# The sign of converted float64 weights: written by a Prelu in place of operations of its own

## The chip, the cores and the metric

The kernel runs on 1 core of a Trainium2 chip, in one launch. Times are device microseconds (us): the median of 3 runs is 590.7 us (590.65 to 592.02). A profile was taken of one execution; its span, from the first instruction to the last, is 589.4 us. Engines are named as in the profile: PE is TensorE (PEld its weight loads), DVE is VectorE, ACT is ScalarE, POOL is GpSimd, SP is SyncE, which issues most DMAs.

## The reference

Three layers follow one another. All sizes are fixed, and the two MLPs' weights arrive as float64.

```python
# 1: retention with decay, batch 2, 8 heads, 768 positions, 64 channels, blocks of 64
intra = einsum(qb, kb) * Dmask ; intra = einsum(intra, vb)
inter = einsum(qb * lam_pow, kv_state)
out   = intra + inter
kv_state = lam**64 * kv_state + einsum(kb * rev_pow, vb)
# 2: MLP, x is 1536 x 512, w_in 512 x 2048, w_out 2048 x 512
h = x @ w_in ; r = maximum(h, 0) ; x = (r * r) @ w_out
# 3: gated MLP, w_gate and w_val 512 x 1536, w_out 1536 x 512
out = (sigmoid(x @ w_gate) * (x @ w_val)) @ w_out
```

## The kernel before, in words

**Weights.** The weights are cut into 68 units of 128 x 512 numbers: 2 for each of the 16 blocks of the first MLP (w_in, w_out), 3 for each of the 12 blocks of the second (gate, value, w_out). A unit arrives as float64, as pairs of 32-bit words (tile `raw`, 512 KB). [...]

A conversion has an ACT part, `conv_act` (L145), and a DVE part, `conv_dve` (L168). ACT scales the high word, read as float32, by 2^-112 with a Copy (tile `j`, L155): that moves the exponent so that three bits are free below the sign. It also scales the low word into an integer `r`, the bits that the high word lacks (L163). DVE shifts `j` left by 3 into `m` (L186), which loses the sign, and at the end adds `m` and `r` into the float32 unit `u` (L181). For the sign there are two ways:

- Without `sign`: DVE takes the top bit of `j` and joins it to `m` with one more operation over the unit (L189). Where the unit is to be negated (`flip`, the gate and value units of even blocks of the second MLP) the shift also sets the top bit (L196) and the join is an exclusive or.
- With `sign=True`: DVE has no such operation. ACT writes `r` in two halves instead: the low 16 bits from the low word (L159) and the high 16 bits as a float16 made from the high word scaled by 2^-60 (L161), which holds the sign alone. 16 of the 68 units are converted in this way, all of them early.

**Stages.** One stream of instructions per engine, in the order in which the code is written (a manual schedule). First retention, 4 of 6 chunk pairs, with PE kept busy by filler matmuls at its start (to 43 us). Then `step_1` for 16 blocks f of the first MLP on the first 512 tokens (to 150 us), with the other retention pairs between. Then the first MLP's other tokens, as seven products per 2 x 2 block (L678, to 224 us), its second matmul (L1066, to 311 us), `step_2` for 12 blocks of the second MLP on the first 512 tokens (to 410 us), and the rest, again by seven products (L678, L995).

PE keeps precision by splitting: every factor is a rounded high part and a low rest (`whi`, `wlo`), so a product is 3 groups of 4 matmuls of 512 columns. In `step_1(f)` PE runs `mm_in(f)` (12 matmuls, L472: whi by xh, then wlo by xh, then whi by xl) and `mm_out(f-1)` (12, L486: gh by whi, gh by wlo, gl by whi). ACT rounds the next block's two units (`whi`, L458), squares the activated block (`r`, L503; `g`, L504), rounds it (`gh`, L516), and does the ACT part of two conversions. DVE makes the rests (`wlo`, L460; `gl`, L518) and the DVE part of two conversions; `weave` (L205) puts the conversion's operations and these rests on DVE's queue in turn, one of each. From f = 8 on, work for the next stage is mixed in at places set by a running clock of PE's planned work: `combine_x` makes sums and splits of the activations (`t` L577, `xch` L561, `xcl` L564), `prepare_a` those of weights (`as` L642 to L645, `ah` L651, `al` L657).

Conversions run in retention and `step_1` (34 units on ACT), beside the second matmul of the first MLP (24, `convert`) and in the first part of `step_2` (the rest). Every conversion's last operation leads to a store, and every `conv_act` with `more` to the next load of `raw`, both on SP's queue.

Of the kernel before, what the change touches and what calls it, by code (L numbers as in the profile page):

```python
# [7 lines left out]
F32 = mybir.dt.float32  # L8
F32R = mybir.dt.float32r
AF = mybir.ActivationFunctionType  # L10
ALU = mybir.AluOpType
# [27 lines left out]
def retention_moe_kernel(  # L39
# [24 lines left out]
    nc = tc.nc  # L64
# [6 lines left out]
    I32 = mybir.dt.int32  # L71
# [11 lines left out]
    def unit(name, dt=F32):  # L83
        return up.tile([P, 512], dt, tag="u", name=name)
# [8 lines left out]
    def at(pos, fn):  # L93
        agenda.append((pos, len(agenda), fn))
# [40 lines left out]
    def load_w(n):  # L135
        for _ in range(min(n, len(to_load))):
            ph, f, u = key = to_load.pop(0)
            t = wp.tile([P, 512, 2], I32, tag="w", name="raw")
            src = (w1 if ph == 1 else w2)[f, u].bitcast(I32)
            nc.sync.dma_start(out=t, in_=src.rearrange("p (n two) -> p n two", two=2))  # L140
            raw_t[key] = t

    ready = []

    def conv_act(more=True, sign=False):  # L145

        if not to_conv or to_conv[0] not in raw_t:
            return  # L150
        key = to_conv.pop(0)
        t = raw_t.pop(key)
        j = unit("j")
        r = unit("r", I32)
        nc.scalar.activation(j, t[:, :, 1].bitcast(F32), AF.Copy, scale=2.0**-112)  # L155
        low = t[:, :, 0].bitcast(mybir.dt.uint32)
        if sign:
            parts = r.bitcast(mybir.dt.int16).rearrange("p (n two) -> p n two", two=2)
            nc.scalar.activation(parts[:, :, 0], low, AF.Copy, scale=2.0**-29)  # L159
            top = parts[:, :, 1].bitcast(mybir.dt.float16)  # L160
            nc.scalar.activation(top, t[:, :, 1].bitcast(F32), AF.Copy, scale=2.0**-60)  # L161
        else:
            nc.scalar.activation(r, low, AF.Copy, scale=2.0**-29)  # L163
        ready.append((key, j.bitcast(I32), r, sign))
        if more:
            load_w(1)

    def conv_dve():  # L168

        if not ready:  # L170
            return []
        key, j, r, sign = ready.pop(0)
        ph, f, u = key
        flip = ph == 2 and u < 2 and f % 2 == 0
        m = unit("m", I32)
        w = unit("u")
        if ph == 1:
            w_t[key] = w

        def last():  # L180
            nc.vector.tensor_tensor(out=w.bitcast(I32), in0=m, in1=r, op=ALU.add)  # L181
            n_stored[0] += 1
            at(clock[0] + 4.0, lambda: nc.sync.dma_start(out=w32[ph][f, u], in_=w))

        ops = [
            lambda: nc.vector.tensor_scalar(  # L186
                out=m, in0=j, scalar1=3, scalar2=None, op0=ALU.logical_shift_left
            ),
            lambda: nc.vector.scalar_tensor_tensor(  # L189
                out=m, in0=j, scalar=-(2**31), in1=m, op0=ALU.bitwise_and,  # L190
                op1=ALU.bitwise_xor if flip else ALU.bitwise_or,
            ),
            last,
        ]
        if flip:
            ops[0] = lambda: nc.vector.tensor_scalar(  # L196
                out=m, in0=j, scalar1=3, scalar2=-(2**31),
                op0=ALU.logical_shift_left, op1=ALU.bitwise_or,
            )
        if sign:  # L200
            assert not flip
            ops.pop(1)
        return ops

    def weave(a, b):  # L205

        for i in range(max(len(a), len(b))):
            for ops in (a, b):
                if i < len(ops):
                    ops[i]()  # L210

    def run(ops):
        weave(ops, [])
# [79 lines left out]
    def new_xr():  # L293
        for t in (1, 2):
            xr[t] = xp.tile([P, 4, TB], F32, tag=f"xr{t}", name=f"xr{t}")
# [156 lines left out]
    def split_w(ph, f):  # L452
        ops = []
        for u in range(2 if ph == 1 else 3):
            src = w_t.pop((ph, f, u))
            hi = unit("whi", F32R)
            lo = unit("wlo", F32R)
            nc.scalar.copy(hi, src)  # L458
            ops.append(
                lambda lo=lo, src=src, hi=hi: nc.vector.tensor_tensor(  # L460
                    out=lo, in0=src, in1=hi, op=ALU.subtract
                )
            )
            split_t[ph, f, u] = (hi, lo)
        return ops
# [26 lines left out]
    def stage_a(ph, f):  # L492
        accs = []
        for u in range(ph):
            accs.append(bank())
            mm_in(accs[u], split_t.pop((ph, f, u)))
        return accs
# [23 lines left out]
    def stage_b(ph, f, g):  # L521
        nf = NF1 if ph == 1 else NF2
        if f == 0:
            accs[ph] = [bank() for _ in range(4)]
        mm_out(accs[ph], split_t.pop((ph, f, ph)), g, f == 0, f == nf - 1)
# [565 lines left out]
    def attend(half):  # L1091
        what, k = SLOTS.get(half, (None, 0))
        if what == "scores":
            att_scores(k)
            passed(SCORES)
            if k < NCH - 1:
                load("q5 v5" if k == 10 else "q12 v11")
            return lambda: (att_keys(k), run(att_prep(k)))
        if what == "out":
            pair = PAIRS[k]  # L1100
            for c in pair:
                att_decay(c, nc.gpsimd)
            att_uv(pair)
            att_out(pair)
            for c in pair:
                kv_t.pop(c)
            passed(REST)
            return lambda: [f() for c in pair for f in att_state(c) + att_x(c)]
        return lambda: None

    def step_1(f):

        acc = stage_a(1, f)
        n = PACE[f] if len(to_conv) + len(ready) > 3 * NF2 else 0
        weave(conv_dve() if n > 0 else [], split_w(1, f + 1) if 0 < f < NF1 - 1 else [])
        if rest:
            rest.pop()()
        if n > 0:
            conv_act()
        attend(2 * f)()  # L1120
        if prev:
            stage_b(*prev.pop())
        last = attend(2 * f + 1)
        gs, ops = split_g(elem(1, f, acc))
        weave(conv_dve() if n > 1 else [], ops)
        for m in range(1, n):
            if m > 1:
                run(conv_dve())
            conv_act(True, f < 10)
        last()  # L1130
        prev.append((1, f, gs))

# [24 lines left out]
    with tc.manual_schedule():  # L1157
# [4 lines left out]
        warm_up(WARM)  # L1162
        decay_rows()
        new_xr()
        conv_act(False, True)
        load(NEXT)
        run(conv_dve())
        conv_act(False, True)
        run(conv_dve())
        att_scores(0)  # L1170
        warm_up(FILL[0])
# [6 lines left out]
        ops = [op for c in PAIRS[0] for op in att_prep(c)]  # L1178
        run([ops[1], ops[0], ops[2], ops[3]])
        query(SEQ_CH + 1, qk_t[SEQ_CH + 1][:, 0, :])  # L1180
        for k in range(LEAD):
            pair, nxt = PAIRS[k], PAIRS[k + 1]
            att_out(pair)
            if k:
                att_uv(pair)
            if not k:
                x = [f for c in pair for f in att_x(c)]
                att_scores(nxt[0])
                att_uv(pair)
                att_scores(nxt[1])  # L1190
            elif k + 1 < LEAD:
                for c in nxt:
                    att_scores(c)
            else:
                att_scores(nxt[0])
            for c in pair:
                kv_t.pop(c)
            load(LOOP[k])
            if k < 2:
                conv_act(False, True)  # L1200
            for c in pair:
                run(att_state(c))
            if k + 1 < LEAD:
                for c in nxt:
                    att_decay(c, nc.scalar)
                more = [op for c in nxt for op in att_prep(c)]
                for c in nxt:
                    att_keys(c)
                if not k:
                    run(x + more)  # L1210
                else:
                    run(more)
                    x = [f for c in pair for f in att_x(c)]
                    if k + 2 == LEAD:
                        run(split_w(1, 0))
                    run(x)
                if k < 2:
                    run(conv_dve())
                else:
                    conv_act(False, True)  # L1220
            else:
                run([f for c in pair for f in att_x(c)])
                run(split_w(1, 1))
                conv_act(False, True)
                run(conv_dve())
                att_keys(nxt[0])
                late = att_prep(nxt[0])
                rest.append(lambda: run(late))
            flush()
# [120 lines left out]
```

## Time and profile before

| | |
|---|---|
| median of 3 runs | 590.7 us |
| span of the profiled execution | 589.4 us |
| PE busy | 576.1 us, 98% |
| DVE busy | 474.0 us, 80% |
| ACT busy | 366.9 us, 62% |
| POOL busy | 47.6 us, 8% |
| chain that ended last, by engine | PE 80%, DVE 9%, ACT 4%, DMA 3%, issue 3% |
| TensorE clock granted | 1.00 in every slice |

The profiled execution has no total of its own beside its span; 590.7 - 589.4 = 1.3 us is what lies around the span against the median run. The chain is the work that ended last, followed back from the end: its shares say which engine was waited for, which busy time alone does not. A wait is put down to the engine and line whose signal came last.

### The profile page before, as it was taken

To read this page: it belongs to the slowest core of one execution; us is meant where nothing else is said; L and a number is where in the kernel's file an instruction comes from. 1 tells how busy PE (TensorE), PEld (TensorE's weight loads), DVE (VectorE), ACT (ScalarE), POOL (GpSimd) and SP (SyncE) were. 2 spreads that over 40 slices of the span, in tenths; PEclk is the share of its full clock that TensorE was granted. 3 is DMA by queue.
4 is the path that set the end of the run, shared out by engine and by line. 5 is a ranking of instruction groups with operands and counts; after the bars stand their busy time and mean duration, and the time that the engine had idled before them with its cause. 6 is when DMAs were issued, how large, how long until landed. Compare 5 with 4: busy or idle time off the path is not lost.

```text
span 589.4 us, 9045 instructions
## 1 busy us (share of the span) xinstructions
PE 576.1 (98%) x3172; PEld 471.7 (80%) x3172; DVE 474.0 (80%) x732; ACT 366.9 (62%) x605; POOL 47.6 (8%) x48
## 2 busy tenths in 40 slices
PE   9899999999999999999999999999999999999996
PEld 8788888767888888888888887888887888878885
DVE  2789896899788868988777788985678877789974
ACT  4679999997656557756467645544545554475470
POOL 1751100000000000000000000022012110000000
PEclk9999999999999999999999999999999999999999
DMA  7999896783253297999978878994547678488681
GB/s 260 413 405 376 311 310 216 226 293 105 71 189 134 108 304 263 413 408 413 404 273 289 307 246 272 339 305 102 174 89 205 187 229 233 153 320 307 205 304 72
DMA packets 69008, 150.83 MB, mean 256 GB/s; under 512 B 7137, under 2 KB 14305, under 8 KB 68962
## 3 DMA queue, kind: packets, MB, share of 16 engines
q1 hardware_dynamic: 64656, 144.34, 68.8%
q0 software_dynamic: 3360, 3.93, 4.5%
q10 hardware_dynamic: 946, 1.97, 1.0%
q8 instruction: 25, 0.41, 0.3%
q14 instruction: 21, 0.17, 0.1%
HBM read 106.43 MB, written 42.21 MB: 252 GB/s over the span
## 4 chain that ended last, share of the span: by engine, by line
PE 80%; DVE 9%; ACT 4%; DMA 3%; issue 3%; POOL 0%; DVEq 0%; SPq 0%; ACTq 0%
PE p L678 28%; PE p L1066 15%; PE p L472 15%; PE p L486 10%; PE p L995 8%; DMA gr<-gs 2%; PE p L315 2%; PE p L400 2%; DMA decay<-w_dram 1%; DVE at L350 1%; PE p L383 1%; DVE m L189 1%; PE p L411 1%; DVE gq L862 1%; DVE xcl L564 1%
## 5 line engine op out<-in xcount | busy, mean ns | idle before, releaser
L678 PE MATMUL p<-xch,ah 128*128 128x512 f32 x280 | 110.0, 393 | 1.0 <-ACT s L687 0.5
L678 PE MATMUL p<-xcl,ah 128*128 128x512 f32 x280 | 109.1, 390 | 0.0
L678 PE MATMUL p<-xch,al 128*128 128x512 f32 x280 | 109.1, 390 | 0.0
L678 PEld LDWEIGHTS p<-xch,ah 128*128 128x128 f32 x280 | 52.6, 188 | 15.3 <-ACT s L687 3.5
L687 ACT COPY s<-p 128x512 f32<-128x512 f32 x60 | 35.2, 588 | 43.8 <-PE p L678 43.7
L678 PEld LDWEIGHTS p<-xch,al 128*128 128x128 f32 x280 | 52.6, 188 | 11.0
L678 PEld LDWEIGHTS p<-xcl,ah 128*128 128x128 f32 x280 | 52.6, 188 | 10.6
L995 PE MATMUL p<-gq,wq 128*128 128x512 f32 x252 | 57.7, 390 | 1.0 <-DVE wq L952 1.0
L692 DVE TENSOR_TENSOR c<-p,s 128x512 f32<-128x512 f32 x60 | 41.2, 687 | 19.4 <-PE p L678 19.0
L995 PEld LDWEIGHTS p<-gq,wq 128*128 128x128 f32 x252 | 47.2, 188 | 11.4 <-DVE wq L952 1.6
L155 ACT ACTIVATE j<-raw 128x512 f32<-128x512 f32 x68 | 45.7, 672 | 12.9 <-issue 5.3
L181 DVE CUSTOM_DVE_ANT_0 u<-m,r 128x1024 uint16<-128x1024 uint16 x68 | 49.6, 729 | 4.7 <-ACT r L161 1.7
L460 DVE TENSOR_TENSOR wlo<-u,whi 128x512 fp32r<-128x512 f32 x68 | 46.0, 708 | 6.2 <-ACT whi L458 5.0
L1066 PE MATMUL p<-g2h,whi 128*128 128x512 f32 x128 | 49.8, 389 | 0.0
L1066 PE MATMUL p<-g2l,whi 128*128 128x512 f32 x128 | 49.8, 389 | 0.0
L1066 PE MATMUL p<-g2h,wlo 128*128 128x512 f32 x128 | 49.8, 389 | 0.0
L472 PE MATMUL p<-xh,wlo 128*128 128x512 f32 x160 | 43.8, 395 | 3.8 <-DVE wlo L460 3.8
L472 PE MATMUL p<-xh,whi 128*128 128x512 f32 x160 | 43.2, 392 | 0.0
L472 PE MATMUL p<-xl,whi 128*128 128x512 f32 x160 | 42.8, 390 | 0.0
L163 ACT ACTIVATE r<-raw 128x512 int32<-128x512 uint32 x52 | 34.5, 663 | 8.2 <-PE p L1066 4.9
L472 PEld LDWEIGHTS p<-xh,wlo 128*128 128x128 f32 x160 | 29.4, 188 | 12.6 <-DVE wlo L460 6.9
L458 ACT CAST whi<-u 128x512 fp32r<-128x512 f32 x68 | 37.9, 615 | 0.5 <-PE p L472 0.5
(129 smaller groups left out, 1048.3 us busy)
## 6 DMA issues: line engine op xcount, KB each, us to landing
raw<-in_w SPq DMA_DIRECT2D x68, 512.0 KB, 6.4
w<-u SPq DMA_DIRECT2D x68, 256.0 KB, 5.1
u<-w SPq DMA_DIRECT2D x52, 256.0 KB, 5.1
a<-w SPq DMA_DIRECT2D x20, 512.0 KB, 4.1
g<-g SPq DMA_DIRECT2D x32, 256.0 KB, 4.4
g<-g SPq DMA_DIRECT2D x16, 512.0 KB, 7.6
gr<-gs SPq DMA_DIRECT2D x24, 256.0 KB, 5.6
kv<-in_kv SPq DMA_DIRECT2D x11, 512.0 KB, 10.4
```

What stands on the lines that cost most here:

```text
L155: nc.scalar.activation(j, t[:, :, 1].bitcast(F32), AF.Copy, scale=2.0**-112)
L163: nc.scalar.activation(r, low, AF.Copy, scale=2.0**-29)
L181: nc.vector.tensor_tensor(out=w.bitcast(I32), in0=m, in1=r, op=ALU.add)
L458: nc.scalar.copy(hi, src)
L460: lambda lo=lo, src=src, hi=hi: nc.vector.tensor_tensor(out=lo, in0=src, in1=hi, op=ALU.subtract)
L472: nc.tensor.matmul(acc, lhsT=a[:, kk * P : (kk + 1) * P], rhs=b[:, kk, :], start=i == 0, stop=i == 11,)
L486: nc.tensor.matmul(acc[e], lhsT=a[:, e * P : (e + 1) * P], rhs=b, start=first and i == 0, stop=last and i == 2,)
L678: nc.tensor.matmul(acc, lhsT=w[:, col, kk * P : (kk + 1) * P], rhs=x[:, kk, :], start=start and i == 0, stop=stop and i == 5, skip_group_c ...
L687: nc.scalar.copy(s, acc)
L692: nc.vector.tensor_tensor(out=c, in0=acc, in1=s, op=ALU.add)
L995: nc.tensor.matmul(acc[k], lhsT=a[:, wn], rhs=block_of(b, gn), start=first and n == 0, stop=last and n == 3 * len(group) - 1,)
L1066: nc.tensor.matmul(acc[e, t], lhsT=a[:, e * P : (e + 1) * P], rhs=b[:, t, :], start=first and i == 0, stop=last and i == 2,)
```

## The change

The scaling of the high word becomes a Prelu: for words at or above zero it multiplies by the scale, for negative ones by the scale and by `alpha`. With `alpha` = 2^32 the exponent of a negative word lands 32 higher, so that after the shift left by 3 the top bit is set, and the rest of the bits are the same as for a positive word. For units to be negated the two are exchanged (scale 2^-80, `alpha` 2^-32). DVE's join (L189) goes for all 52 units that had it, ACT's third operation (L161) for the 16 that had that, and with it the strided 16-bit write (L159) becomes the plain one (L163). `conv_dve` returns two operations, so in `weave` the last one (`u`) stands one place earlier.

```diff
-    def conv_act(more=True, sign=False):
+    def conv_act(more=True):
...
-        nc.scalar.activation(j, t[:, :, 1].bitcast(F32), AF.Copy, scale=2.0**-112)
+        ph, f, u = key
+        flip = ph == 2 and u < 2 and f % 2 == 0
+        nc.scalar.activation(
+            j, t[:, :, 1].bitcast(F32), AF.Prelu,
+            scale=2.0**-80 if flip else 2.0**-112, alpha=2.0**-32 if flip else 2.0**32,
+        )
         low = t[:, :, 0].bitcast(mybir.dt.uint32)
-        if sign:
-            parts = r.bitcast(mybir.dt.int16).rearrange("p (n two) -> p n two", two=2)
-            nc.scalar.activation(parts[:, :, 0], low, AF.Copy, scale=2.0**-29)
-            top = parts[:, :, 1].bitcast(mybir.dt.float16)
-            nc.scalar.activation(top, t[:, :, 1].bitcast(F32), AF.Copy, scale=2.0**-60)
-        else:
-            nc.scalar.activation(r, low, AF.Copy, scale=2.0**-29)
-        ready.append((key, j.bitcast(I32), r, sign))
+        nc.scalar.activation(r, low, AF.Copy, scale=2.0**-29)
+        ready.append((key, j.bitcast(I32), r))
...
-        ops = [
+        return [
             lambda: nc.vector.tensor_scalar(
                 out=m, in0=j, scalar1=3, scalar2=None, op0=ALU.logical_shift_left
             ),
-            lambda: nc.vector.scalar_tensor_tensor(
-                out=m, in0=j, scalar=-(2**31), in1=m, op0=ALU.bitwise_and,
-                op1=ALU.bitwise_xor if flip else ALU.bitwise_or,
-            ),
             last,
         ]
```

Line numbers fall by 15 in the changed kernel behind this place (L460 becomes L445); `j` is L157, `r` L162, the shift L184, `u` L179. No instruction of PE, POOL or SP moves. DVE's queue has 660 rows before and 608 after, ACT's 501 and 485; both have two ACT_TABLE_LOADs, one at the start and one ahead of the first Sigmoid.

The first place is ACT's queue in `step_1(8)`, where a conversion of the early kind stands (r_1519 of the unit j_1518, between the rounding gh of block 8 and the whi of block 10). Before:

```order
L503 ACTIVATE r_1505<-p_1458 128x512
L504 ACTIVATE g_1506<-r_1505 128x512
L516 CAST gh_1509<-g_1506 128x512
L155 ACTIVATE j_1518<-raw_1386 128x512
L159 ACTIVATE r_1519<-raw_1386 128x512
L161 ACTIVATE r_1519<-raw_1386 128x512
L458 CAST whi_1542<-u_1444 128x512
```

The same place on ACT after:

```order
L488 ACTIVATE r_1483<-p_1436 128x512
L489 ACTIVATE g_1484<-r_1483 128x512
L501 CAST gh_1487<-g_1484 128x512
L157 ACTIVATE j_1495<-raw_1366 128x512
L162 ACTIVATE r_1496<-raw_1366 128x512
L443 CAST whi_1518<-u_1424 128x512
```

Everything behind the conversion moves up by one instruction.

The second place is DVE's queue in `step_1(13)`, from block 12's rest gl_1791 over the sums `as` of the next stage's weights to the two rests `wlo` of block 14 and the conversion u_1828 woven with them. Before:

```order
L186 TENSOR_SCALAR m_1793<-j_1766 128x512
L518 TENSOR_TENSOR gl_1791<-g_1787,gh_1790 128x512
L189 SCALAR_TENSOR_TENSOR m_1793<-j_1766,m_1793 128x512
L181 ISA u_1794<-m_1793,r_1767 128x1024
L642 TENSOR_TENSOR as_1822<-a_1710 128x256
...
L186 TENSOR_SCALAR m_1827<-j_1799 128x512
L460 TENSOR_TENSOR wlo_1830<-u_1723,whi_1829 128x512
L189 SCALAR_TENSOR_TENSOR m_1827<-j_1799,m_1827 128x512
L460 TENSOR_TENSOR wlo_1833<-u_1754,whi_1832 128x512
L181 ISA u_1828<-m_1827,r_1800 128x1024
```

The same place on DVE after:

```order
L184 TENSOR_SCALAR m_1763<-j_1736 128x512
L503 TENSOR_TENSOR gl_1761<-g_1757,gh_1760 128x512
L179 ISA u_1764<-m_1763,r_1737 128x1024
L627 TENSOR_TENSOR as_1791<-a_1682 128x256
...
L184 TENSOR_SCALAR m_1796<-j_1768 128x512
L445 TENSOR_TENSOR wlo_1799<-u_1695,whi_1798 128x512
L179 ISA u_1797<-m_1796,r_1769 128x1024
L445 TENSOR_TENSOR wlo_1802<-u_1725,whi_1801 128x512
```

Both joins are gone, and the conversion's last operation (u_1797 after, u_1828 before) now stands ahead of the second `wlo`, where the join stood.

## Rows read from the trace of the kernel before

**Rows 1.** Windows: stretch, PE, PEld, DVE, ACT, POOL busy us (count), clock, DMA.

```profile
43.00:95.00 52.00, 52.00 (x392) 42.34 (x388) 47.02 (x78) 48.69 (x85) 7.16 (x6) 1.00 0.89 322
95.00:141.50 46.50, 43.17 (x191) 32.88 (x183) 40.57 (x66) 42.18 (x70) 0.00 (x0) 1.00 0.67 224
```

**Rows 2.** Chain that ended last, in retention: start us, us, what.

```profile
23.75 1.28 DVE at L350 x2
```

**Rows 3.** Timeline, PE: start us, us, engine, line, operation, tiles, shape, count.

```profile
106.21 1.07 PE L472 MATMUL p<-xh,whi 128*128 128x512 f32 x4
111.65 1.07 PE L472 MATMUL p<-xh,whi 128*128 128x512 f32 x4
144.56 0.39 PE L678 MATMUL p<-xch,ah 128*128 128x512 f32 x1
```

**Rows 4.** Waits from 95 to 141.5 us: total us, times, longest.

```profile
PEld p L472 <- DVE wlo L460: 5.4, 5, 2.0
ACT xch L561 <- DVE t L577: 1.2, 2, 0.9
```

**Rows 5.** Groups by line and shape, whole span: busy us, mean ns, idle before.

```profile
L155 ACT ACTIVATE j<-raw 128x512 f32<-128x512 f32 x68 | 45.7, 672 | 12.9 <-issue 5.3 <-DMA raw<-in_w 3.3 <-PE p L1066 2.4
L458 ACT CAST whi<-u 128x512 fp32r<-128x512 f32 x68 | 37.9, 615 | 0.5 <-PE p L472 0.5
L687 ACT COPY s<-p 128x512 f32<-128x512 f32 x60 | 35.2, 588 | 43.8 <-PE p L678 43.7
L163 ACT ACTIVATE r<-raw 128x512 int32<-128x512 uint32 x52 | 34.5, 663 | 8.2 <-PE p L1066 4.9 <-PE p L486 2.9 <-PE p L472 0.3
L651 ACT CAST ah<-as 128x1024 fp32r<-128x1024 f32 x20 | 20.9, 1046 | 1.1 <-DVE as L645 1.1
L159 ACT ACTIVATE r<-raw 128x512 int16<-128x512 uint32 x16 | 12.6, 786 | 0.2 <-PE p L486 0.2
L161 ACT ACTIVATE r<-raw 128x512 f16<-128x512 f32 x16 | 12.4, 772 | 0.0
L503 ACT ACTIVATE r<-p 128x512 f32<-128x512 f32 x16 | 9.4, 589 | 0.0
L367 ACT ACTIVATE tt<-S,G 128x64 f32<-128x64 f32 x24 | 6.0, 335 | 3.7 <-DVE S L430 3.7
```

**Rows 6.** Groups by line, 95 to 141.5 us.

```profile
L155 ACT ACTIVATE j<-raw 128x512 f32<-128x512 f32 x12 | 8.1, 673 | 0.0
L161 ACT ACTIVATE r<-raw 128x512 f16<-128x512 f32 x2 | 1.5, 771 | 0.0
L189 DVE SCALAR_TENSOR_TENSOR m<-j,m 128x512 int32<-128x512 int32 x9 | 6.2, 684 | 0.0
```

**Rows 7.** Timeline, ACT in `step_1`.

```profile
102.42 0.78 ACT L161 ACTIVATE r<-raw 128x512 f16<-128x512 f32 x1
103.06 1.12 ACT L458 CAST whi<-u 128x512 fp32r<-128x512 f32 x2
...
122.39 1.05 ACT L561 CAST xch<-t 128x1024 fp32r<-128x1024 f32 x1 [0.86 <-DVE t L577]
...
133.57 0.62 ACT L516 CAST gh<-g 128x512 fp32r<-128x512 f32 x1
```

**Rows 8.** Timeline, DVE and the PE that waits for it.

```profile
115.32 0.69 DVE L518 TENSOR_TENSOR gl<-g,gh 128x512 fp32r<-128x512 f32 x1 [0.45 <-ACT gh L516]
...
132.48 0.68 DVE L460 TENSOR_TENSOR wlo<-u,whi 128x512 fp32r<-128x512 f32 x1
...
133.22 0.74 PE L472 MATMUL p<-xh,wlo 128*128 128x512 f32 x2 [1.62 <-DVE wlo L460]
```

**Rows 9.** Timeline, PE and DVE in `step_2`.

```profile
349.24 1.07 PE L472 MATMUL p<-xh,whi 128*128 128x512 f32 x4
...
358.41 1.89 DVE L460 TENSOR_TENSOR wlo<-u,whi 128x512 fp32r<-128x512 f32 x3
...
361.12 1.08 PE L472 MATMUL p<-xh,whi 128*128 128x512 f32 x4
```

More of the change, by code (lines that the diff above doesn't have):

```diff
@@ L171, in conv_dve @@
             return []
-        key, j, r, sign = ready.pop(0)
+        key, j, r = ready.pop(0)
         ph, f, u = key
-        flip = ph == 2 and u < 2 and f % 2 == 0
         m = unit("m", I32)
@@ L188, in conv_dve @@
             ),
-            lambda: nc.vector.scalar_tensor_tensor(
-                out=m, in0=j, scalar=-(2**31), in1=m, op0=ALU.bitwise_and,
-                op1=ALU.bitwise_xor if flip else ALU.bitwise_or,
-            ),
             last,
         ]
[L195 to L203, printed above, removed]
     def weave(a, b):
@@ L1128, in step_1 @@
                 run(conv_dve())
-            conv_act(True, f < 10)
+            conv_act(True)
         last()
@@ L1164, in retention_moe_kernel @@
         new_xr()
-        conv_act(False, True)
+        conv_act(False)
         load(NEXT)
         run(conv_dve())
-        conv_act(False, True)
+        conv_act(False)
         run(conv_dve())
@@ L1199, in retention_moe_kernel @@
             if k < 2:
-                conv_act(False, True)
+                conv_act(False)
             for c in pair:
@@ L1219, in retention_moe_kernel @@
                 else:
-                    conv_act(False, True)
+                    conv_act(False)
             else:
@@ L1223, in retention_moe_kernel @@
                 run(split_w(1, 1))
-                conv_act(False, True)
+                conv_act(False)
                 run(conv_dve())
```

## The prediction

> **What bounds the kernel now.** I read the stages first (windows), then PE's starts (timeline), then who was waited for (waits), then ACT's and DVE's queues where PE waits. PE is busy 576 of 589 us, so only time that PE loses can be won. Where the conversions run, it loses time in two stretches.
>
> The pace of PE without loss: `mm_in` of block 10 starts at 106.21 us, that of block 11 at 111.65, 24 matmuls later [rows 3]. That is 5.44 us per block, 0.227 us per matmul, 2.72 us for 12. From 111.65 us to the first product of the next stage at 144.56 lie 5 `mm_in` and 5 `mm_out`, 120 matmuls, 27.2 us at that pace; they took 32.9. **PE loses 5.7 us here**, nearly all of it waiting for `wlo` [rows 3, 4]. In 43 to 95 us it loses nothing, with DVE busy for 47.0 and ACT for 48.7 of 52 us [rows 1]; what is saved there buys no time.
>
> The second stretch is in `step_2`. From 349.24 to 361.12 us there are four thirds of its block: 48 matmuls, 10.9 us at the pace, 11.9 taken. **1.0 us is lost**, most of it at the `wlo` of 358.41 [rows 9].
>
> In retention the chain goes through DVE's products with the decay [rows 2], which wait for scores from PE; none of the five conversions of that stage is in it, so I count nothing there. Between 144.6 and 349 us, and from 361 us to the end, PE waits for no part of a conversion.
>
> **Part by part.** *The join on DVE.* 52 instructions go, at 0.684 us each [rows 6]; 35.6 us of DVE's time, of which nine lie in the first stretch.
>
> *The third operation on ACT.* 16 go. The next start behind one is 0.64 us later (102.42 to 103.06 [rows 7]), and the write ahead of it gets 0.12 us shorter (786 to 663 ns [rows 5]): 0.76 us per unit. Two of these units are converted after 95 us [rows 6]; the one at 102.42 and the second near 109 give 1.5 us.
>
> *The Prelu itself.* No Prelu is in the trace. Nearest rows: a Relu from PSUM takes 589 ns and a copy from PSUM 588 [rows 5] (L503 and L687), so another function costs nothing there, and I take the 672 ns of today's Copy on line 155 [rows 5]. Above: an operand that each row of the tile fetches. L367 has one, 335 ns for 64 columns; the casts of 512 and 1024 columns (615, 1046) give 0.842 ns per column and 184 ns fixed, so 64 columns would take 238, and the operand costs 97 ns [rows 5]. Below: 57 ns less, if the Prelu got down to the cast's 615. For the 12 conversions of the first stretch [rows 6] that is +1.2 and -0.7 us of ACT's time.
>
> The Trainium skill (ScalarE: Activation LUTs, What ACT_TABLE_LOAD costs) states 93 ns for an operand held in a tile and none for a number in the instruction; the trace's 97 ns agrees. The diff gives `alpha` as a number, so by that rule the term is 0; if the engine treats it as a tile's operand all the same, it is 12 times 93 ns, 1.1 us, and the sum below 1.1 us smaller.
>
> *The place of `u`.* It stands ahead of the second `wlo` now. That `wlo` is the rest of the block's output weights, which `mm_out` uses a whole `mm_in` later; and 0.73 us of `u` in place of 0.69 of the join costs it 0.04 us. `u` waits for an `r` that ACT wrote ahead of the `whi` that the first `wlo` needs. No wait is added. Stores and loads on SP follow `u` and ACT as before, as many of them.
>
> *First stretch, ACT.* ACT is the engine to watch: of 46.5 us it is busy for 42.2 [rows 1], the rest being a little at its start and end, and two waits for DVE's `t`, 1.2 us together [rows 4]. So from 95 us on its queue sets the pace. The rounding `gh` of block 13 starts at 133.57 and ends at 134.2. Earlier by: 1.5 us for the two operations, and 0.86 for the wait at 122.39, which goes since DVE is then far ahead [rows 7]. (The other wait, 0.35 us, stays: ACT gets there earlier by as much as DVE.) Together 2.3 to 2.4 us; `gh` is there at 131.9.
>
> *First stretch, DVE.* From the `gl` at 115.32 to the `wlo` of block 14 at 132.48 DVE never rests, and five joins stand between, each worth the 0.61 us to the next start or a little more [rows 6, 8]: 3.1 us. The `gl` waits for ACT's `gh` and comes 1.4 earlier with ACT. So that `wlo` starts at 128.0 and is done at 128.7. PE would want it 4 matmuls behind the start of that `mm_in`: 111.65 + 6 x 2.72 = 127.97, + 0.91 = 128.9. Just in time, and the 1.62 us wait at 133.22 [rows 8] is gone; the earlier `wlo`s have more room.
>
> *What is late next.* After 7 groups of 12, at 111.65 + 19.04 = 130.69 us, PE wants `gh` of block 13 for `mm_out(13)`, and gets it at 131.9: it waits 1.2 us, for ACT. Behind it `mm_out(13)`, `mm_in(15)` and `mm_out(14)` run without a stop (ACT's last conversion is over), 8.16 us, to 140.1 us, and the next stage starts then; 144.56 before. The first stretch gives 4.5 us, less 0.1 for the restart: **4.4**.
>
> *Second stretch.* DVE alone is late there, by 1.0 us, and three joins stand ahead of the last `wlo` between 348 and 356 us, worth 1.9 us: **1.0**, all that is lost.
>
> *Sum.* 5.4 us off the span of 589.4: 584.0. With the 1.3 us that lie between span and median, 590.7 - 5.4 = **585.3 us**.
>
> **Rivals.**
> - *All the loss goes.* ACT's delay at `gh` of block 13 is only 1.2 us, less if the Prelu is a little shorter or ACT has 0.76 us more by a third early unit. Then 5.7 + 1.0 = 6.7: 584.0 us. Against: the ACT queue has next to no idle time left.
> - *The Prelu costs what a fetched operand costs.* ACT has 1.2 us more to do in the first stretch, and as its queue paces PE, PE gets it all: 5.4 - 1.2 = 4.2, 586.5 us. For: Prelu has one number more than Copy uses. Against: the 589 and 588 of [rows 5].
> - *Only ACT's own advance counts.* If some wait of DVE on ACT that I left out paces PE at each block, PE advances by 2.3 us as ACT does, and 1.0 in the second stretch: 587.4 us.
> - *It makes no difference*: the chain that PE waits for closes again over something else, a load of `raw` above all, that comes in time only because PE is late today; 590 us. Against: between 95 and 141 us no wait is for a DMA.
> - *Slower: the Prelu takes a second pass.* If the negative side cost another pass over the tile, each `j` would take 0.57 us more. In the first stretch 12 of them put 6.8 us on the engine that paces it; from 43 to 95 us 17 of them put 9.7 us on ACT, where 9 early units give back 6.8 and only 3.3 us are idle [rows 1], so some 1.6 us of it reaches PE. 585.3 + 6.8 + 1.6 = 593.7 us. It turns slower from 5.4 / 12 = 0.45 us per Prelu. For: nothing but that no Prelu is in the trace; against: Relu, which also tells the signs apart, at a copy's price.
>
> That the change does not do what it says is no rival: the joins and the third operations are out of the two queues, and there are as many table loads as before.
>
> **How the numbers follow.** Forecast 0.52; all the loss 0.13; fetched operand 0.15; ACT's advance only 0.10; no difference 0.06; second pass 0.04. The range reaches from all the loss, 583.8, to beyond ACT's advance, 588.0: it leaves out the last two and slips of the others. What a measurement can tell from no change is 0.3%, 1.8 us, so faster means under 588.9: the first four, 0.90; within, 0.06; slower, 0.04.
>
> **What would show it.** Right: no group for L189 or L161; `j` at 0.66 to 0.69 us; in 95 to 137 us PE's waits for `wlo` under 1 us, and one wait of about 1 us for `gh` near 131; the first L678 near 140 us; no wait for `wlo` near 355. DVE some 36 us less busy, ACT some 14. Wrong: `j` over 0.75 us; PE still waiting for `wlo` for 2 us or more in that stretch; or a new wait behind 140 us, for weights or activations that came early enough only because PE was late.

## The result, and the profile after

| | before | changed |
|---|---|---|
| median | 590.9 us (590.65 to 592.02, 4 runs) | 584.3 us (584.02 to 587.14, 4 runs) |
| span of the profiled execution | 589.4 us | 582.4 us |
| DVE busy | 474.0 us | 436.8 us |
| ACT busy | 366.9 us | 356.5 us |

The ratio is 0.9901, with a 95% interval from 0.9877 to 0.9924 (the two medians alone give 0.9888): 1.0% faster. The forecast was 585.3 us, its range 583.8 to 588.0.

The profiled executions can be laid side by side: PE runs the same matmuls in the same order, so at each landmark one reads how far the changed kernel is ahead.

| landmark | before | changed | ahead | gained since |
|---|---|---|---|---|
| first product of retention with the decay (L400, now L385) | 18.09 | 17.06 | 1.03 | 1.03 |
| `mm_in` of block 11 | 111.65 | 110.55 | 1.10 | 0.07 |
| first product of the next stage (L678, now L663) | 144.56 | 139.10 | 5.46 | 4.36 |
| `step_2`, the first `mm_in` of the second stretch | 349.24 | 343.52 | 5.72 | 0.26 |
| its end | 361.12 | 354.40 | 6.72 | 1.00 |
| end of the span | 589.4 | 582.4 | 7.0 | 0.3 |

The first landmark in both, before and then changed:

```profile
18.09 2.33 PE L400 MATMUL p<-at,kv 128*64 128x128 f32 x32 [1.81 <-DVE at L350]
```

```profile
17.06 1.09 PE L385 MATMUL p<-at,kv 128*64 128x128 f32 x16 [1.24 <-DVE at L335]
```

The groups of the changed kernel by line and shape (busy us, mean ns, idle before) answer to [rows 5]:

```profile
L157 ACT ACTIVATE j<-raw 128x512 f32<-128x512 f32 x68 | 45.6, 671 | 17.3 <-issue 6.5 <-DMA raw<-in_w 5.4 <-PE p L1051 4.0
L162 ACT ACTIVATE r<-raw 128x512 int32<-128x512 uint32 x68 | 45.0, 662 | 1.6 <-PE p L457 0.9 <-PE p L1051 0.7
L184 DVE TENSOR_SCALAR m<-j 128x512 int32<-128x512 int32 x68 | 28.6, 420 | 2.4 <-PE p L1051 1.6 <-PE p L471 0.5 <-ACT j L157 0.4
```

A Prelu takes 671 ns where the Copy took 672: it costs no more than the Copy. There is no group for a join or a third ACT operation. The stages, in the columns of [rows 1]:

```profile
43.00:95.00 52.00, 52.00 (x390) 42.39 (x389) 40.03 (x69) 42.02 (x75) 7.98 (x7) 1.00 0.93 340
95.00:141.50 46.50, 45.56 (x201) 37.20 (x200) 40.78 (x65) 43.99 (x73) 0.00 (x0) 1.00 0.60 215
```

From 43 to 95 us DVE and ACT are 7 us less busy each, and PE has gained nothing: it was full there before (52.00 of 52 us in [rows 1] too). From 95 us on PE does more in the same time (45.6 us busy, not 43.2). The waits in that stretch answer to [rows 4] (total us, times, longest):

```profile
DVE gl L503 <- ACT gh L501: 4.6, 5, 2.2
...
PEld p L471 <- ACT gh L501: 1.4, 1, 1.4
PE p L471 <- ACT gh L501: 0.9, 1, 0.9
ACT xch L546 <- DVE t L562: 0.3, 1, 0.3
PEld p L457 <- DVE wlo L445: 0.2, 1, 0.2
```

The waits of the weight loads for `wlo` fell from 5.4 us to 0.2, those of ACT for DVE's `t` from 1.2 to 0.3. DVE waits for ACT now, and PE has one wait left, for `gh`. Its place in the timeline, on ACT and on PE:

```profile
126.95 0.67 ACT L157 ACTIVATE j<-raw 128x512 f32<-128x512 f32 x1
127.53 0.66 ACT L162 ACTIVATE r<-raw 128x512 int32<-128x512 uint32 x1
128.09 0.82 ACT L636 CAST ah<-a 128x768 fp32r<-128x768 f32 x1
128.81 0.59 ACT L488 ACTIVATE r<-p 128x512 f32<-128x512 f32 x1
129.44 0.63 ACT L489 ACTIVATE g<-r 128x512 f32<-128x512 f32 x1
130.10 0.62 ACT L501 CAST gh<-g 128x512 fp32r<-128x512 f32 x1
```

```profile
110.55 1.07 PE L457 MATMUL p<-xh,whi 128*128 128x512 f32 x4
...
126.89 1.07 PE L457 MATMUL p<-xh,whi 128*128 128x512 f32 x4
127.80 1.12 PE L457 MATMUL p<-xh,wlo 128*128 128x512 f32 x4
128.75 1.08 PE L457 MATMUL p<-xl,whi 128*128 128x512 f32 x4
130.77 1.21 PE L471 MATMUL p<-gh,whi 128*128 128x512 f32 x4 [0.94 <-ACT gh L501]
131.82 1.09 PE L471 MATMUL p<-gh,wlo 128*128 128x512 f32 x4
...
139.10 0.39 PE L663 MATMUL p<-xch,ah 128*128 128x512 f32 x1
```

`mm_out(13)` would have begun at 128.75 + 0.91 = 129.66 us and began at 130.77, when `gh` was there. ACT has no gap in these rows. The `wlo` of block 14, for which PE lost 1.62 us before, is no longer late:

```profile
126.98 0.69 DVE L445 TENSOR_TENSOR wlo<-u,whi 128x512 fp32r<-128x512 f32 x1
```

Up to the `mm_in` at 126.89 PE has kept its pace of 2.72 us per 12 matmuls: (126.89 - 110.55) / 6 = 2.72. In `step_2` no wait is left; the rows answer to [rows 9]:

```profile
343.52 1.07 PE L457 MATMUL p<-xh,whi 128*128 128x512 f32 x4
...
351.68 1.07 PE L457 MATMUL p<-xh,whi 128*128 128x512 f32 x4
352.58 1.07 PE L457 MATMUL p<-xh,wlo 128*128 128x512 f32 x4
...
354.40 0.84 PE L457 MATMUL p<-xh,whi 128*128 128x512 f32 x3
```

### The profile page after: what moved, and what is told of

Same layout as the page of the kernel before. It is cut to its first block, busy times and chain, and to the rows that moved or that the text cites. A ratio compares the mean times of both kernels' runs of the same rounds, so it can differ in the third digit from the quotient of the medians.

```text
span 582.4 us, 8970 instructions
## 1 busy us (share of the span) xinstructions
PE 572.5 (98%) x3172; PEld 471.9 (81%) x3172; DVE 436.8 (75%) x680; ACT 356.5 (61%) x589; POOL 48.5 (8%) x48
## 4 chain that ended last, share of the span: by engine, by line
PE 80%; ACT 6%; DMA 6%; DVE 4%; issue 2%; SPq 0%; POOL 0%; DVEq 0%; ACTq 0%
PE p L663 28%; PE p L457 15%; PE p L1051 15%; PE p L471 10%; PE p L980 8%; DMA gr<-gs 3%; DMA kv<-in_kv 2%; DMA qk<-in_qk 1%; PE p L300 1%; PE p L385 1%; ACT j L157 1%; ACT whi L443 1%; DVE gq L847 1%; ACT ah L636 1%; PE p L396 1%
## 5 line engine op out<-in xcount | busy, mean ns | idle before, releaser
L663 PE MATMUL p<-xch,ah 128*128 128x512 f32 x280 | 109.9, 392 | 1.0 <-ACT s L672 0.5
L663 PE MATMUL p<-xcl,ah 128*128 128x512 f32 x280 | 109.0, 389 | 0.0
L663 PE MATMUL p<-xch,al 128*128 128x512 f32 x280 | 109.0, 389 | 0.0
L663 PEld LDWEIGHTS p<-xch,ah 128*128 128x128 f32 x280 | 52.5, 188 | 15.0 <-ACT s L672 3.2
L663 PEld LDWEIGHTS p<-xch,al 128*128 128x128 f32 x280 | 52.6, 188 | 11.0
L663 PEld LDWEIGHTS p<-xcl,ah 128*128 128x128 f32 x280 | 52.6, 188 | 10.6
L157 ACT ACTIVATE j<-raw 128x512 f32<-128x512 f32 x68 | 45.6, 671 | 17.3 <-issue 6.5
L445 DVE TENSOR_TENSOR wlo<-u,whi 128x512 fp32r<-128x512 f32 x68 | 45.1, 694 | 12.3 <-ACT whi L443 12.0
L179 DVE CUSTOM_DVE_ANT_0 u<-m,r 128x1024 uint16<-128x1024 uint16 x68 | 50.0, 735 | 2.9 <-PE p L457 0.6
L162 ACT ACTIVATE r<-raw 128x512 int32<-128x512 uint32 x68 | 45.0, 662 | 1.6 <-PE p L457 0.9
L611 POOL DMA_DIRECT2D as<-w x6 | 5.6, 934 | 368.8 <-DMA as<-w 305.4
```

The costliest lines, as they stand in the source:

```text
L157: nc.scalar.activation(j, t[:, :, 1].bitcast(F32), AF.Prelu, scale=2.0**-80 if flip else 2.0**-112, alpha=2.0**-32 if flip else 2.0**32,)
L445: lambda lo=lo, src=src, hi=hi: nc.vector.tensor_tensor(out=lo, in0=src, in1=hi, op=ALU.subtract)
L663: nc.tensor.matmul(acc, lhsT=w[:, col, kk * P : (kk + 1) * P], rhs=x[:, kk, :], start=start and i == 0, stop=stop and i == 5, skip_group_c ...
```

## The experiments

Theory: PE's loss from 111 to 145 us is shared by two queues; the joins on DVE and the third operations on ACT must both go, and what is left is ACT's own. The loss in `step_2` is the joins' alone. The rivals were ACT alone, DVE alone, and DVE's busy time as such. The first four kernels were timed against before on one chip (before: 591.0 us, 590.33 to 591.9, 15 runs); the repeats at the end ran on another.

**The DVE operation put back (join_kept).** The Prelu and the shorter ACT part stay; a join that ors nothing in stands in its old place in the 52 units.

```diff
+        if unit_no >= 26 or unit_no > 5 and unit_no % 2 == 0:
+            ops.insert(1, lambda: nc.vector.scalar_tensor_tensor(
+                out=m, in0=j, scalar=0, in1=m, op0=ALU.bitwise_and, op1=ALU.bitwise_or,
+            ))
```

> The changed kernel with one DVE operation over the unit put back where the join was, in all 52 units (it ors nothing in): Prelu and the shorter ACT part stay. My theory (ACT and DVE share the gain of the first stretch, the joins alone make that of the second): of the 5.7 us lost from 111.65 to 144.56 only about 1.4 come back, none of the 1.0 in step_2; about 1.4 us faster than before, 589.5 us, or about 588.4 if the 1.0 us that the changed kernel is early at 17 us belongs to the change. Rival, ACT alone: 585.4 us. Rival, DVE alone: 590.7 us. DVE busy about 472 us.

Measured: 590.4 us (589.18 to 591.7, 11 runs), ratio 0.9988 (0.9979 to 0.9997). From the first product of retention to the first of the next stage it takes 125.96 us, before 126.47, changed 122.04: the stretch gained 0.5 us, and I had expected 1.4. The stretch in `step_2` gained nothing, as expected. The time is above what I expected too, and lies nearer to the 590.7 us of "DVE alone" than to it; what decides is the stretch, which repeats within 0.1 us (below). The same place in before, then in join_kept, with what each waited for:

```profile
111.17 1.22 DVE L577 TENSOR_TENSOR t<-xr,xr 128x1024 f32<-128x1024 f32 x1
112.42 1.04 ACT L561 CAST xch<-t 128x1024 fp32r<-128x1024 f32 x1 [0.35 <-DVE t L577]
```

```profile
108.56 1.22 DVE L555 TENSOR_TENSOR xcl<-xr,xch 128x1024 fp32r<-128x1024 f32 x1
109.70 1.22 DVE L568 TENSOR_TENSOR t<-xr,xr 128x1024 f32<-128x1024 f32 x1
110.83 0.42 DVE L184 TENSOR_SCALAR m<-j 128x512 int32<-128x512 int32 x1
110.95 1.05 ACT L552 CAST xch<-t 128x1024 fp32r<-128x1024 f32 x1 [1.12 <-DVE t L568]
111.17 0.68 DVE L451 TENSOR_TENSOR wlo<-u,whi 128x512 fp32r<-128x512 f32 x1
...
111.91 0.77 PEld L463 LDWEIGHTS p<-xh,wlo 128*128 128x128 f32 x4 [0.52 <-DVE wlo L451]
```

ACT did come earlier, and spent half of its 1.5 us waiting for DVE's `t`: 1.12 us at this place, 0.35 before. DVE, with the joins back, is 1.47 us earlier here, 0.9 of it by an earlier start (17.19 us, not 18.09) and 0.6 by its own, and gains no more after it; the wait of 1.6 us for the `wlo` of block 14 is back too. PE's waits for `wlo` from 95 to 141.5 us (total us, times, longest):

```profile
PE p L463 <- DVE wlo L451: 2.6, 4, 1.6
```

So ACT's 1.5 us are worth 0.5 alone and more only together with the joins. ACT alone is out; so is DVE alone, by these 0.5 us and by the next run.

**The ACT part put back (act_kept).** No joins, but the 16 early units are converted by three ACT operations and a Copy as before.

```diff
+        if ph == 1 and 2 * f + u < 26 and (2 * f + u < 6 or u == 1):
+            nc.scalar.activation(j, t[:, :, 1].bitcast(F32), AF.Copy, scale=2.0**-112)
+            parts = r.bitcast(mybir.dt.int16).rearrange("p (n two) -> p n two", two=2)
+            nc.scalar.activation(parts[:, :, 0], low, AF.Copy, scale=2.0**-29)
+            top = parts[:, :, 1].bitcast(mybir.dt.float16)
+            nc.scalar.activation(top, t[:, :, 1].bitcast(F32), AF.Copy, scale=2.0**-60)
+        else:
...
```

> The changed kernel with the old ACT part (three operations, a Copy instead of the Prelu) in the 16 early units; no joins. My theory: ACT's queue comes to gh of block 13 1.5 us later than in the changed kernel, PE waits there 2.7 us instead of 1.3, the first stretch gives 2.9 us instead of 4.4, step_2 gives its 1.0: 585.8 us. Rival, DVE alone: as the changed kernel, 584.3 us. On the start: if the early third operations on ACT are what made the first 18 us 1.0 us longer, the first product of retention (L385) is back at 18.1 us and the time at 586.8 us; if that was a matter of when loads land, it stands anywhere from 17.0 to 18.1.

Measured: 585.8 us (585.4 to 587.11, 5 runs), ratio 0.9913 (0.9901 to 0.9926). From the first product of retention to the first of the next stage it takes 123.47 us (140.60 - 17.13): 3.0 us gained where the changed kernel gains 4.4, as expected. ACT is later by 1.49 us at the same `gh`, 0.07 of it by the start:

```profile
131.59 0.62 ACT L508 CAST gh<-g 128x512 fp32r<-128x512 f32 x1
```

```profile
130.24 1.07 PE L464 MATMUL p<-xl,whi 128*128 128x512 f32 x4
132.26 0.98 PE L478 MATMUL p<-gh,whi 128*128 128x512 f32 x3 [0.96 <-ACT gh L508]
```

In both kernels the next stage begins 8.4 us behind the end of that `gh` (140.60 - 132.21 and 139.10 - 130.72), so its delay is what the stretch loses. The place of PE's wait was not as expected: I had said 2.7 us at this `gh`, and PE waits 0.96 there, as in the changed kernel (0.94). It had lost the rest on the way. From 95 us on, weight loads wait for `gh` three times, not once, and near 48 us one waits 0.41 us, which costs PE 0.3; in the profile of before, PE comes to that place 0.9 us later and doesn't wait. Waits from 95 to 141.5 us:

```profile
PEld p L478 <- ACT gh L508: 2.4, 3, 1.4
```

This kernel began retention at 17.13 us with the old ACT part in its first five conversions, so these alone do not make a start late.

**Joins where PE loses nothing (joins_idle).** The same neutral join as in join_kept, in 40 units that are converted from 43 to 93 us and from 224 to 345 us.

```diff
+        if 33 <= unit_no < 65 or 5 < unit_no < 22 and unit_no % 2 == 0:
```

> The changed kernel with the neutral DVE operation in 40 of the 52 units, those converted from 43 to 93 us (8) and from 224 to 345 us (32): 27 us of DVE's time. My theory: no cost, PE waits for no conversion there, 584.3 us. Rival, that DVE's time as such counts: 40/52 of the gain goes, about 589.4 us. In between (a backlog of DVE carried into step_2): up to 585.3 us.

Measured: 585.8 us (585.14 to 587.14, 4 runs), ratio 0.9907 (0.9892 to 0.9922). DVE's time is back; by stage, joins_idle first, then the changed kernel:

```profile
43.00:95.00 52.00, 52.00 (x387) 42.29 (x387) 47.91 (x79) 42.97 (x75) 7.13 (x7) 1.00 0.90 327
224.00:345.00 121.00, 121.00 (x535) 100.22 (x534) 100.00 (x157) 77.21 (x124) 0.00 (x0) 1.00 0.93 346
```

```profile
224.00:345.00 121.00, 121.00 (x535) 100.19 (x535) 80.82 (x128) 76.66 (x123) 0.00 (x0) 1.00 0.95 351
```

27 us more on DVE (7.9 and 19.2), and PE is full in both windows either way. From the first product of retention to the first of the next stage it takes 122.28 us, 0.24 more than in the changed kernel, and from there to the end of the second stretch 215.34, against 215.30: 0.3 us for 40 joins. The median, though, is 1.5 us above that of the changed kernel, above the expected 584.3 and the upper 585.3. The one profiled execution is the slowest of its four runs (587.1 us), and its 2.8 us over the changed kernel's span lie for the most part where no join stands: retention began at 18.30 us, the latest of all (1.24), and 1.3 more went behind 356 us, 0.9 of that in PE's waits for the last stage's weights `wq`. For the median no profile exists; the changed kernel itself took 585.7 and 585.3 us in its repeats below. A join is worth what PE waits for it, and DVE's 80% says nothing of that.

**Two conversions moved behind the wait (two_later).** Units 32 and 33, converted in `step_1(13)` though needed only in `step_2`, go to the conversions beside the second matmul.

```diff
-PACE = (2, 2, 2, 2, 2, 2, 2, 2, 2, 2, 2, 2, 2, 2, 1, 0)
+PACE = (2, 2, 2, 2, 2, 2, 2, 2, 2, 2, 2, 2, 2, 1, 0, 0)
...
-        if n > 0:
+        if n > 0 and f < 13:
             conv_act()
```

> The changed kernel with the two last conversions of step_1 (units 32 and 33, those of step 13) moved to the conversions beside the second matmul. What PE still waits for in the changed kernel is ACT at gh of block 13, 1.2 us; the j and r of unit 32 stand ahead of that gh and take 1.1 us. My theory: gh comes 1.1 us earlier, 583.2 us. Rival: the wait is not ACT's own work but that of block 13's sums behind PE: no change, 584.3. Price: all later conversions come two places later, the last ones near 355 us instead of 348; if PE waits for weights there, up to 1 us lost.

Measured: 583.4 us (583.08 to 583.6, 4 runs), ratio 0.9869 (0.9856 to 0.9883): the fastest here. ACT and PE at the place of the last wait:

```profile
127.05 0.84 ACT L636 CAST ah<-a 128x768 fp32r<-128x768 f32 x1
127.79 0.59 ACT L488 ACTIVATE r<-p 128x512 f32<-128x512 f32 x1
128.41 0.63 ACT L489 ACTIVATE g<-r 128x512 f32<-128x512 f32 x1
129.08 0.62 ACT L501 CAST gh<-g 128x512 fp32r<-128x512 f32 x1
```

```profile
128.86 1.07 PE L457 MATMUL p<-xl,whi 128*128 128x512 f32 x4
129.77 1.20 PE L471 MATMUL p<-gh,whi 128*128 128x512 f32 x4
```

The `j` and `r` ahead of `gh` are gone, `gh` comes 1.02 us earlier, and PE goes on without a wait: the stretch to the first product of the next stage takes 120.97 us, 1.07 less than in the changed kernel. The price feared in `step_2` did not come: from there to the end of the second stretch it is 215.35 us, against 215.30.

**The start, again.** 1.03 of the 7.0 us were won before 18 us, where I had counted nothing. Both kernels were profiled twice more, unchanged.

> The kernel before once more, for its start. The first product of retention with the decay (L400) began at 18.09 us in the profile of before, at 17.06 in that of the changed kernel. If that 1.0 us is a matter of when the first loads land (theory A), it begins anywhere from 17.0 to 18.3 us here, early in one or both of the two repeats of before, and the repeats of the changed kernel are spread over the same stretch. If it comes with the change (theory B), before begins at 18.0 to 18.1 us each time.

> The changed kernel once more, for its start (L385). Theory A: from 17.0 to 18.3 us, as before. Theory B: 17.0 to 17.1 us each time. From that product to the first L663 the stretch is as in the first profile, 122.0 us, within 0.1.

> Before, second repeat: as for the first. From the first product of retention (L400) to the first L678 it takes 126.5 us, within 0.1, whenever it begins.

> The changed kernel, second repeat: as for the first, a start of the first product with the decay from 17.0 to 18.3 us by theory A, at 17.0 to 17.1 us by theory B.

| | time | retention begins | from there to the next stage |
|---|---|---|---|
| before, first profile | | 18.09 | 126.47 |
| before_1 | 590.9 | 17.75 | 126.55 |
| before_2 | 591.0 | 18.02 | 126.49 |
| changed, first profile | 584.3 | 17.06 | 122.04 |
| after_1 | 585.7 | 17.87 | 122.03 |
| after_2 | 585.3 | 17.40 | 122.04 |

The stretch behind the start is the same to 0.1 us in every execution of a kernel; the start is not. That of the changed kernel varies by 0.8 us, and with the other kernels of this section, which have its early ACT and DVE instructions or the old ones, from 17.06 to 18.30. Neither expectation holds: before is not at 18.0 to 18.1 each time, and it is never early. On average it begins at 17.95 us and the changed kernel at 17.44, so half of that 1.0 us is the difference of two executions, and whether the other half belongs to the change stays open: three are too few. The medians do not tie it to the early instructions. What they gain on before outside the time from the first product of retention to the end of the second stretch is 0.9 us in the changed kernel, 0.9 in two_later and 1.0 in act_kept, which has the old early ACT part, but 0.1 in join_kept (11 runs) and -0.2 in joins_idle, which have the changed kernel's. On the other chip the two repeats of the changed kernel lie 5.3 us under the median of three runs of before (590.2, 590.9, 591.0), no more than the forecast's 5.4.

## Why the prediction was right

*The first stretch* was said to lose 5.7 us, to give 4.4 and to keep a wait of 1.2 us at `gh` of block 13. It gave 4.36; the wait was 1.1 us, at that `gh`, which was forecast for 131.9 us and ended at 130.72, 1.1 of that being the earlier start. The two queues came as forecast as well: less those 1.1 us, the `wlo` of block 14 was due at 126.9 us and began at 126.98, and ACT's wait of 0.86 us for `t` went while that of 0.35 stayed (0.3). The steps behind it were tried: that ACT's two third operations are worth 1.5 us at that `gh` (act_kept: 1.42 later, the start aside, and 1.43 lost in the stretch), that the joins are needed for the rest (join_kept), and that ACT's last wait is its own queue (two_later: taken away, 1.07). The two shares do not add up: without the joins alone the stretch gained 3.0 us, with ACT's shorter part alone 0.5, with both 4.4.

*The second stretch* was said to give 1.0 us by the joins alone, and gave 1.00; with the joins kept, nothing.

*The Prelu's price* was taken as that of the Copy, between -57 and +97 ns: -1. The fetched operand and the second pass are out.

*What was said to cost or give nothing* did so: the joins from 43 to 93 and from 224 to 345 us (joins_idle: 0.3 us for 40 of them), `u` ahead of the second `wlo` (0.2 us of waits for `wlo` are left), the conversions' part in retention (act_kept with the old one takes 25.1 us from its first product to the first `mm_in`, before and changed 25.0).

*What was wrong in passing.* ACT was to be some 14 us less busy and is 10.4. The groups of `r` and the third operation did lose 14.5 us of duration (59.5, now 45.0), but rows that follow each other on ACT overlap: the `j` at 126.95 lasts 0.67 us and the `r` behind it begins 0.58 later. In the rival of the second pass, the 1.6 us that reach PE do not follow: 9.7 less 6.8 is 2.9 us, under the 3.3 that are idle. The rival was out by 671 ns all the same.

*What the numbers missed.* The median came 1.0 us under the forecast: 6.4 us under the 590.7 from which the forecast counts, where 5.4 were said. The profiled executions are 7.0 us apart, and show where: 5.4 in the two stretches, 1.03 at the start, 0.26 at a wait near 153 us, 0.3 at the end and 0.07 from 18 to 112 us; none of the last four was foreseen. They are further apart than the medians because the profiled execution of before was longer than the median one by some 0.5 us: the 15 runs of before that give both time and span show 1.7 to 1.9 us between them, where the prediction took 1.3 from two different executions. The forecast does not hang on that, since it takes 5.4 from the median. The start is the largest of the four, and is not shown to come from the change; in the two repeats at 585.7 and 585.3 us, close to the forecast, it was 0.8 and 0.3 us later. So the two stretches are explained, and the last 1.0 us is not. The steps of reasoning that the runs put right were outside the forecast, in the expectations: in join_kept ACT's time alone was worth 0.5, not 1.4, since ACT then waits for DVE; in act_kept the loss was of the size expected, but PE's wait at `gh` of block 13 was 0.96 us, not 2.7.

## What to carry to other kernels

An operation taken off a busy queue is worth what the bound engine waits for behind it: here 12 of 52 DVE operations (joins_idle put the other 40 back) and, by the prediction's count, 2 of 16 on ACT made nearly all of 5.4 us, 48 us of engine time saved in all. The 2 of 16 were not tried by themselves; act_kept put back all 16. To size such a change, take the bound engine's pace from a stretch without waits, count what each stretch takes beyond it, and follow both queues on paper to the first place where the other one is late; the remaining wait then names the next edit, as it did here (two conversions moved, 1.1 us). Where two engines feed each other, neither's saving can be read alone.

## What the runs showed of the hardware

The first copy of the decay table by DVE takes 0.63 us with POOL idle, and up to 1.46 us beside a POOL multiplication. The first profile of before and the changed kernel:

```profile
15.12 1.04 POOL L331 TENSOR_TENSOR kd<-kv,W 128x512 f32<-128x512 f32 x1 [9.31 <-DMA kv<-in_kv]
15.19 1.46 DVE L1175 COPY D<-decay 128x512 f32<-128x512 f32 x1 [1.69 <-DMA decay<-w_dram]
```

```profile
13.71 1.04 POOL L316 TENSOR_TENSOR kd<-kv,W 128x512 f32<-128x512 f32 x1 [7.89 <-DMA kv<-in_kv]
14.97 0.63 DVE L1160 COPY D<-decay 128x512 f32<-128x512 f32 x1 [2.85 <-DMA decay<-w_dram]
```

Which of the two it is depends on which load lands first, `kv` or the table: before_1, with POOL started 0.84 us ahead, had 0.69 us, before_2, with 0.25, had 1.28. In all ten profiled executions the copy grows with what is left of the multiplication (1.04 us) when it starts: 0.62 or 0.63 us in the four with under 0.05 us left, 0.68 to 0.71 with 0.2, 0.83 with 0.34, 1.28 with 0.79, 1.46 with 0.97. ACT's copy of another part, which starts at the same moment, takes 1.12 to 1.14 us in all ten. This compares executions; no run moved the multiplication. The copy makes up to 0.8 us of a start that varies by 1.2.

The multiplication itself, which waits for `kv`, began at 14.78 to 15.12 us in the three executions of before and at 13.71 to 14.50 in the seven of the other kernels, act_kept among them. Why `kv` lands later in before stays open.
